# Expert weights split by ScalarE and VectorE alone

## Chip, core and metric

The kernel runs on one core of a Trainium2 chip. The metric is the device time of one execution in microseconds, the median of three runs. The engines are TensorE (PE; its weight loads are listed as PEld), VectorE (DVE), ScalarE (ACT), GpSimd (POOL) and SyncE (SP), which here issues most of the DMAs.

## What is computed

Three layers follow each other:

```python
# 1. attention of 2 batches, 8 heads, 768 tokens, 64 dims; a token sees those of its cluster
mask = q_assign[:, :, :, None] == k_assign[:, :, None, :]
scores = np.where(mask, scale * np.matmul(q, k.transpose(0, 1, 3, 2)), -1000000000.0)
attn_out = softmax(scores) @ v
# 2. dense layer, 1536 tokens, 512 -> 2048 -> 512
h = np.maximum(x @ w_in, 0.0)
x = h * h @ w_out
# 3. experts: N, D, E, F = (1536, 512, 8, 1024)
do_compute = x @ w_skip > 0
e_idx = np.argmax(xc @ w_gate, axis=1)          # xc: the selected tokens
h = np.maximum(xc[mask] @ w1[e], 0.0)           # mask: the tokens of expert e
y[mask] = gate_w[mask, None] * (h @ w2[e])
out[do_compute] = xc + y
```

The weights of layer 3, `w1` (8 x 512 x 1024) and `w2` (8 x 1024 x 512), are float32.

## The kernel before

Products are made in PE's float32r format from exact parts: an operand x is split into hi (x rounded to that format) and lo = x - hi, and a product is the sum of hi·hi, hi·lo and lo·hi. Every operand thus costs a cast and a subtract on some other engine. In the names, `wih` and `wil` are the two parts of a piece of w1, `woh` and `wol` those of w2; `xh`, `xl` belong to a tile's tokens and `hh`, `hl` to its hidden activations.

The attention and the dense layer come first. The last chunk of the dense layer's tokens is routed (top expert, gate, rank inside the expert; lines 828 to 900), which yields lists of token numbers per expert and the order of the experts. From there the experts' tiles run. There are nine tiles of 128 tokens, 0 to 8: tile 0 (called A) and tile 1 (B) belong to the fullest expert, and each of the others to one other expert. `place` (line 947) loads the number of each expert into a register of SP once it is known, and SP can then load that expert's weights.

A tile u goes through PE in this order (lines 1179 to 1195): `g1(u, 0)`, 12 matmuls of 512 columns for the first half of the hidden features; `g2(u-1, 1)`, the second half of the previous tile's output; four transposes of tile u's hidden activations; `g1(u, 1)`; four transposes of the next tile's tokens; `g2(u, 0)`; four transposes of the second half of the hidden activations. After each group of transposes `parts` (line 1021) splits the result: ACT casts it (line 1028), DVE subtracts (line 1029, one input in PSUM). PE needs the lo part with the third matmul of the next product but one. `finish` (line 1054) has DVE make the output rows (line 1056) and POOL scatter them (line 1058); `gather` (line 1013) has POOL clear a tile and fetch the next but one tile's tokens.

An expert's weights are prepared by `half_weights` (line 746), a generator, called two half-experts at a time (`econvert_to`, line 784) so that they are done about one tile ahead of their use: four tiles of parts of each kind take turns. An expert's weights come in eight loads of 512 KB (`fetch`, line 738), issued by SP into seven staging buffers (`st`, three of them, and `xc`, four pieces of the first two chunks and the later ones) as these come free, that is, when both subtracts of what lay there are done. For each load there is one cast of 128 x 1024 and two subtracts of 128 x 512:

```python
eng = ENGS[p][4 * kind + 2 * n + c // 2]
if eng[0] == "a":
    nc.scalar.copy(out=hi[:, c:c + 2], in_=st)
else:
    hi_pool(hi[:, c:c + 2], st)
for i in range(2):
    (nc.vector if eng[1] == "v" else nc.gpsimd).tensor_tensor(
        out=lo[:, c + i], in0=st[:, i], in1=hi.bitcast(F32)[:, c + i], op=ALU.subtract)
```

These are lines 759 to 766; `hi_pool` (line 137) is a multiplication by 1.0 on POOL. The table that `ENGS` holds (lines 41 to 43 and 728) has a pair of letters for each of an expert's eight loads: the engine of the cast (a for ACT, p for POOL) and that of the subtracts (v for DVE, p for POOL). `ENG0` is for the first expert, `ENG1` for the second, `ENG2` for the other six. PE's order is written out by hand in this part; those of ACT, DVE and POOL are set by the scheduler of the language, which takes the instructions as the program text yields them and moves them by its own estimate of when each can run. Every engine works through its own list strictly in order.

Of the kernel before, what the change touches and what calls it, by code (L numbers as in the profile page):

```python
# [16 lines left out]
BIG = float(2 ** 50)  # L17
# [23 lines left out]
ENG0 = ('av', 'pv', 'av', 'ap', 'av', 'ap', 'ap', 'ap')  # L41
ENG1 = ('av', 'ap', 'av', 'pv', 'av', 'ap', 'av', 'pv')
ENG2 = ('av', 'ap', 'av', 'pv', 'av', 'vv', 'av', 'pv')
# [9 lines left out]
def clustered_attention_moe(  # L53
# [14 lines left out]
    # Token s of a batch sits on partition s // TT of tile s % TT.  # L68
    # Every float32r product is made of exact parts, x = hi + lo.
# [10 lines left out]
    G = 384  # L80
# [26 lines left out]
    # tri[p, m] = 1 where p < m  # L107
    nc.gpsimd.affine_select(out=tri16, in_=ones16, pattern=[[1, 128]], compare_op=ALU.is_gt,
                            fill=0.0, base=0, channel_multiplier=-1)
    # first1[k, m] = 1 where k = m, -1 where k < m in the same group of C, times BIG for k's  # L110
# [17 lines left out]
    # a chunk of G tokens: the attention's output, transposed, then the moe's, by tokens  # L128
# [11 lines left out]
    # parts of the moe's weights, a quarter of the hidden features at a time  # L140
# [10 lines left out]
    def split64(hi, lo, srcs, shape):  # L151
        # float64 words (low, high) to float32, then to its two parts: the exponent is
        # clamped to float32's range and rebased (the shift drops its upper bits); 23 bits
        # of the mantissa stay
        st = stp.tile([128, 512, 2], I32, name="st")
        sv = st.rearrange("p (c f) w -> p c f w", c=shape[0])
        if pace:
            # the load waits for this step's hidden features
            nc.scalar.copy(out=st.bitcast(F32)[:, 0, 0:1], in_=pace[0][:, 0:1])
        for c, src in enumerate(srcs):  # L160
            nc.sync.dma_start(out=sv[:, c], in_=src)
        yield
        lw, hw = st[:, :, 0], st[:, :, 1]
        u = stg.tile([128, 512], I32, name="u")
        l3 = stg.tile([128, 512], I32, name="l3", bufs=1)
        uf = u.bitcast(F32)
        hf = st.bitcast(F32)[:, :, 1]
        nc.scalar.activation(out=uf, in_=hf, func=AF.Abs, scale=2.0 ** -48)
        yield
        nc.vector.tensor_scalar(out=uf, in0=uf, scalar1=2.0 ** -63, scalar2=122880.0 * 2.0 ** -48,  # L170
                                op0=ALU.max, op1=ALU.min)
        yield
        nc.vector.tensor_scalar(out=l3, in0=lw, scalar1=29, scalar2=None, op0=ALU.logical_shift_right)
        yield
        nc.vector.scalar_tensor_tensor(out=l3, in0=hw, scalar=-0x80000000, in1=l3,
                                       op0=ALU.bitwise_and, op1=ALU.bitwise_or)
        yield
        nc.vector.scalar_tensor_tensor(out=u, in0=u, scalar=3, in1=l3,
                                       op0=ALU.logical_shift_left, op1=ALU.bitwise_or)
        yield  # L180
        ufs = uf.rearrange("p (c f) -> p c f", c=shape[0])
        hi_pool(hi, ufs)
        yield
        nc.gpsimd.tensor_tensor(out=lo, in0=ufs, in1=hi.bitcast(F32), op=ALU.subtract)  # L184
        yield
# [28 lines left out]
    # ------------------------------------------------------------------ attention  # L214
    # the operands' tiles, which the moe's tokens take over
# [6 lines left out]
    def x_parts(ch):  # L222
        # of a chunk, in the place of operands
        t = [operand(nm) for nm in (("A", "B") if ch < 3 else ("vs", "vs"))]
        return [(i.rearrange("p t x d -> p (t x d)") if ch == 3 else i.rearrange("p a s -> p (a s)"))
                .rearrange("p (k c) -> p k c", k=KD) for i in t]
# [16 lines left out]
    # the first hidden features' products, which run in the attention's last waits  # L243
# [22 lines left out]
    with ExitStack() as actx:  # L266
# [32 lines left out]
        def centroid():  # L299
            # normalized rows, transposed to [(h % 2, d), (h, c)] with the other head  # L300
            # of a pair zero
# [3 lines left out]
            # rows of even heads go to columns 0-63, of odd heads to 64-127  # L305
# [41 lines left out]
        def split(nm, x, o, hi, lo, heads):  # L347
            # parts by the same partitions, to the operands' rows by DMAs
            rows = slice(64 * heads[0], 128)
            for c in (slice(0, 384), slice(384, 768)):  # L350
                hi_pool(hi[rows, c], x[rows, c])
                nc.gpsimd.tensor_tensor(out=lo[rows, c], in0=x[rows, c], in1=hi.bitcast(F32)[rows, c],
                                        op=ALU.subtract)
            hi, lo = hi.bitcast(F32), lo.bitcast(F32)
            for h in heads:
                r, t = slice(64 * h, 64 * h + 64), o[h].bitcast(F32)
                nc.sync.dma_start(out=t[0:64, 0], in_=hi[r])
                nc.sync.dma_start(out=t[64:128, 0], in_=(lo if nm == "q" else hi)[r])
                nc.sync.dma_start(out=t[0:64, 1], in_=(hi if nm == "q" else lo)[r])

        # Logits by [(q or k, half of the tokens, head, cluster), token], the four blocks of
        # 32 rows at once, then turned.
# [9 lines left out]
        # cluster of each token: one-hot of the first largest logit; the largest ones  # L372
        # are marked and turned, then a later one is taken out by an earlier one
# [25 lines left out]
        # operand rows: 0 or -1 for q, BIG or 0 for k  # L399
# [10 lines left out]
        def split_v(vs, vn):  # L410
            # blocks [hi, lo] of the even head, [lo, hi] of the odd
            for c in range(0, TT, 2):
                c = slice(c, c + 2)
                hi_pool(vs[:, c, 0::3, :], vn[:, c])
                nc.gpsimd.tensor_tensor(out=vs[:, c, 1:3, :], in0=vn[:, c], in1=vs.bitcast(F32)[:, c, 0::3, :],
                                        op=ALU.subtract)
# [3 lines left out]
        def prepare(n):  # L420
            # operands of a pair of heads, in steps of the tensor engine's part and the rest
# [30 lines left out]
        def prepare_first():  # L452
            # the first pair's: the first head's operands come from the engines, for no
            # wait for DMAs; some are in the weights' staging tiles, whose loads then follow
# [80 lines left out]
        def scales(n, c):  # L535
            # 1 / (sum + 1e-9) of the rows, each on the partitions of its head
# [75 lines left out]
        def warm(n):  # L612
            # keeps the tensor engine's clock up through the waits
            if n:
                wm = ps_v.tile([128, G], F32, name="av")
                for _ in range(4 * n):
                    nc.tensor.matmul(out=wm[:, 0:128], lhsT=ones16, rhs=ones16, start=True, stop=True)
# [83 lines left out]
    # ------------------------------------------------------------------ moe  # L701
# [18 lines left out]
    # The experts' tiles of 128 tokens: A and B are of the fullest expert by the tokens  # L720
    # of all chunks but the last, A with those tokens, B with more; then one of every
    # other expert, where expert 0 has the place of the fullest.
# [15 lines left out]
    def fetch():  # L738
        # loads ahead of the conversions, into the free staging tiles
# [6 lines left out]
    def half_weights(p, kind, n, src=None):  # L746
        # two parts of an expert's weights, a half of its hidden features
# [44 lines left out]
    # per token: its number - 4096 in two exact parts, and its gate in three  # L792
# [19 lines left out]
    def turn_x(T):  # L812
        # a tile of tokens goes out, and is turned for its logits
# [14 lines left out]
    def route(ch):  # L828
        # top expert, gate and rank in the expert of the selected tokens of a chunk
# [13 lines left out]
        else:  # L843
            # by [(tile, output), token], the tiles at once, then turned
# [57 lines left out]
    def ranks(ch, base=None):  # L902
        # one-hot of the ranks of a chunk's tokens
# [11 lines left out]
    def slots(ch, sum, so):  # L915
        # per expert and slot: the parts of the token of that rank, 0 if none
# [10 lines left out]
    def index(ix, g, sg):  # L927
        # tokens and gates from their parts
# [4 lines left out]
    def choose():  # L933
        # the fullest expert so far, and the order of the experts
# [19 lines left out]
    def pick(i, sum):  # L954
        # list of the chosen expert
# [5 lines left out]
    def early():  # L961
        # routing of all chunks but the last, where done tells which are finished
# [45 lines left out]
    # ------------------------------------------------------------------ tiles of an expert  # L1008
# [4 lines left out]
    def gather(u):  # L1013
        # A comes from the output's rows: the last chunk's have not gone to xd then
# [6 lines left out]
    def parts(src, name):  # L1021
        # transposed 128-column blocks of src, in two parts
# [39 lines left out]
    # ------------------------------------------------------------------ products of the moe  # L1062
# [66 lines left out]
    def base():  # L1129
        # the last chunk, its second products by tiles of tokens, then tile A  # L1130
# [45 lines left out]
    # ------------------------------------------------------------------ moe2  # L1176
# [20 lines left out]
    # further tiles of tokens, for as many as the experts have  # L1197
# [64 lines left out]
```

## Time and profile before

| what | before |
|---|---|
| median of 3 runs | 709.74 us (709.6 to 710.33) |
| profiled execution | span 706.3 us, 11310 instructions |
| PE, PEld busy | 658.8 us (93%), 569.4 us (81%) |
| DVE busy | 495.7 us (70%), 904 instructions |
| ACT busy | 395.7 us (56%), 825 instructions |
| POOL busy | 313.9 us (44%), 374 instructions |

The profiler's execution is one of its own; it is told by its span, from the first to the last instruction, and no other time is listed for it. It is 3.4 us below the median of the runs, which also holds what lies around the instructions. The page cuts the span in 40 slices of 17.7 us and gives each engine's busy share in tenths:

```profile
PE   7899999999999998999999999999998889869794
DVE  5688999999999997555347655322447789899960
POOL 4545453645635519344334344311002767665510
DMA  6678565565734101212221221012125969878700
```

The attention fills the first 16 or so slices, the dense layer those up to the 30th; the experts' tiles are in the last ten.

### The profile page before, as it was taken

How to read it: one execution, taken by the hardware profiler on the slowest of the kernel's cores; microseconds unless marked ns; L12 is line 12 of the kernel's file. 1: busy time of each engine (PE TensorE's matmuls, PEld its weight loads, DVE VectorE, ACT ScalarE, POOL GpSimd, SP SyncE). 2: the span in 40 equal slices, each digit the busy share in tenths (PEclk: the TensorE clock that was granted, in tenths of full speed). 3: DMA queues.
4: the chain of work that ended last, by engine and by line, in shares of the span. 5: the costliest groups of instructions: out<-in, count | busy, mean ns of one | idle time of the engine just before them, and what ended most of it. 6: DMA issues, size and time to landing. Idle time of an engine off the chain costs nothing. (4 is left out here: it accounts for less than half of the span.)

```text
span 706.3 us, 11310 instructions
## 1 busy us (share of the span) xinstructions
PE 658.8 (93%) x3769; PEld 569.4 (81%) x3769; DVE 495.7 (70%) x904; ACT 395.7 (56%) x825; POOL 313.9 (44%) x374
## 2 busy tenths in 40 slices
PE   7899999999999998999999999999998889869794
PEld 5688888889888887889998999899886768657583
DVE  5688999999999997555347655322447789899960
ACT  6688999989989884444433333223232736444420
POOL 4545453645635519344334344311002767665510
PEclk9999999999999999999999999999999989998998
DMA  6678565565734101212221221012125969878700
GB/s 140 149 167 199 140 148 147 123 148 141 168 95 113 31 0 47 67 60 75 87 75 64 75 82 61 1 45 90 60 85 180 343 217 360 291 242 279 249 26 23
DMA packets 72035, 89.91 MB, mean 127 GB/s; under 512 B 32384, under 2 KB 43584, under 8 KB 71968
## 3 DMA queue, kind: packets, MB, share of 16 engines
q1 hardware_dynamic: 69664, 84.52, 41.0%
q0 software_dynamic: 1440, 3.01, 1.3%
q10 hardware_dynamic: 864, 1.57, 0.6%
q8 instruction: 32, 0.52, 0.3%
q14 instruction: 35, 0.29, 0.1%
HBM read 62.18 MB, written 9.44 MB: 101 GB/s over the span
## 5 line engine op out<-in xcount | busy, mean ns | idle before, releaser
L580 DVE TENSOR_TENSOR pl<-pt,ph 128x384 fp32r<-128x384 f32 x192 | 103.7, 551 | 19.9 <-ACT ph L571 18.4
L557 PE MATMUL pt<-ident,p 128*128 128x128 f32 x576 | 96.6, 277 | 4.9 <-DVE pl L580 3.9
L259 ACT ACTIVATE r<-hps 128x384 f32<-128x384 f32 x62 | 30.4, 491 | 125.7 <-PE hps L252 125.5
L515 PE MATMUL sc<-B,A 80*128 80x384 f32 (+1 forms) x384 | 93.1, 363 | 4.7 <-ACT p L531 1.8
L138 POOL TENSOR_SCALAR hh<-r 128x384 fp32r<-128x384 f32 x62 | 35.0, 564 | 137.7 <-ACT r L260 118.6
L571 ACT CAST ph<-pt 128x384 fp32r<-128x384 f32 x192 | 89.7, 481 | 8.9 <-PE pt L557 8.5
L522 DVE TENSOR_REDUCE nm<-sc 128x1 f32<-128x768 f32 x96 | 91.0, 948 | 2.6 <-PE sc L515 2.6
L531 ACT ACTIVATE p<-sc,nm 128x768 f32<-128x768 f32 x96 | 87.3, 910 | 6.0 <-DVE nm L522 5.5
L262 DVE TENSOR_TENSOR hl<-r,hh 128x384 fp32r<-128x384 f32 x62 | 36.7, 591 | 76.9 <-POOL hh L138 76.9
L557 PEld LDWEIGHTS pt<-ident,p 128*128 128x128 f32 x576 | 70.3, 141 | 20.3 <-DVE pl L580 12.8
L1087 PE MATMUL acc<-woh,hh 128*128 128x512 f32 x186 | 74.2, 399 | 0.0
L1087 PE MATMUL acc<-woh,hl 128*128 128x512 f32 x186 | 73.3, 394 | 0.0
L1087 PE MATMUL acc<-wol,hh 128*128 128x512 f32 x186 | 73.3, 394 | 0.0
L590 PE MATMUL av<-ph,vs 128*128 128x384 f32 x192 | 73.1, 381 | 0.1
L515 PEld LDWEIGHTS sc<-B,A 80*128 80x128 f32 (+1 forms) x384 | 63.3, 191 | 9.9 <-ACT p L531 5.5
L590 PE MATMUL av<-pl,vs 128*128 128x384 f32 x192 | 65.4, 341 | 0.6 <-DVE pl L580 0.6
L252 PE MATMUL hps<-A,wil 128*128 128x384 f32 x184 | 62.0, 337 | 1.8 <-POOL wil L184 1.8
L252 PE MATMUL hps<-A,wih 128*128 128x384 f32 x184 | 62.4, 339 | 0.0
L252 PE MATMUL hps<-B,wih 128*128 128x384 f32 x184 | 62.0, 337 | 0.0
L1087 PEld LDWEIGHTS acc<-woh,hl 128*128 128x128 f32 x186 | 35.0, 188 | 8.0
L1087 PEld LDWEIGHTS acc<-woh,hh 128*128 128x128 f32 x186 | 35.0, 188 | 5.8 <-DVE xc L1095 0.2
L1095 DVE TENSOR_TENSOR xc<-acc,xc 128x512 f32<-128x512 f32 x36 | 24.4, 686 | 21.6 <-PE acc L1087 21.6
(268 smaller groups left out, 1549.4 us busy)
## 6 DMA issues: line engine op xcount, KB each, us to landing
xc<-in_moe_w_dram SPq DMA_DIRECT2D x34, 512.0 KB, 5.0
st<-in_moe_w_dram SPq DMA_DIRECT2D x30, 512.0 KB, 5.2
st<-in_moe_w_in_dram SPq DMA_DIRECT2D x64, 128.0 KB, 3.0
st<-in_moe_w_out_dram SPq DMA_DIRECT2D x16, 512.0 KB, 3.5
A<-hi SPq DMA_DIRECT2D x30, 192.0 KB, 3.1
B<-hi SPq DMA_DIRECT2D x30, 192.0 KB, 3.1
qn<-in_q_dram SPq DMA_DIRECT2D x16, 192.0 KB, 3.2
kn<-in_k_dram SPq DMA_DIRECT2D x16, 192.0 KB, 3.7
```

What stands on the lines that cost most here:

```text
L138: nc.gpsimd.tensor_scalar(out=o, in0=i, scalar1=1.0, scalar2=0.0, op0=ALU.mult, op1=ALU.add)
L252: nc.tensor.matmul(out=hps, lhsT=wi[w][:, c, f * 128:(f + 1) * 128], rhs=xhl[ch][a][:, c], start=(n == 0), stop=(n == 3 * KD - 1))
L259: nc.scalar.activation(out=r, in_=hps, func=AF.Relu)
L262: nc.vector.tensor_tensor(out=hl, in0=r, in1=hh.bitcast(F32), op=ALU.subtract)
L515: nc.tensor.matmul(out=sc[:, c, 0:384], lhsT=A[h][0:kk, a, t * 128:(t + 1) * 128], rhs=Bk[h][0:kk, a, c * 384:(c + 1) * 384], start=(a == ...
L522: nc.vector.tensor_reduce(out=nm_t[i], in_=sc_t[i][:, :, 0:384], op=ALU.max, axis=AX.XY, negate=True)
L531: nc.scalar.activation(out=p, in_=sc[:, :, 0:384], func=AF.Exp, bias=nm, scale=1.0, accum_out=su_t[n, c][:, t, h:h + 1])
L557: nc.tensor.transpose(out=pt[:, c], in_=p_t[i][:, n, c * 128:(c + 1) * 128], identity=ident)
L571: nc.scalar.copy(out=block(i, n)[by_pool].bitcast(F32) if by_pool else block(i, n)[0], in_=pt_t[i, n])
L580: nc.vector.tensor_tensor(out=pl, in0=pt_t.pop((i, n)), in1=ph.bitcast(F32), op=ALU.subtract)
L590: nc.tensor.matmul(out=av, lhsT=vs[:, c, 2 * h:2 * h + 2].rearrange("p x d -> p (x d)"), rhs=r[:, c], start=(c == 0 and i == 0), stop=(c = ...
L1087: nc.tensor.matmul(out=acc, lhsT=h2[a][:, i * 128:(i + 1) * 128], rhs=wo[w][:, f], start=(f == 0 and n == 0), stop=(f == NF - 1 and n == 2))
```

## The change

Every pair in the table becomes `'av'`: ACT makes all casts of the experts' weights and DVE all subtracts.

```diff
-ENG0 = ('av', 'pv', 'av', 'ap', 'av', 'ap', 'ap', 'ap')
-ENG1 = ('av', 'ap', 'av', 'pv', 'av', 'ap', 'av', 'pv')
-ENG2 = ('av', 'ap', 'av', 'pv', 'av', 'vv', 'av', 'pv')
+ENG0 = ('av',) * 8
+ENG1 = ('av',) * 8
+ENG2 = ('av',) * 8
```

(A pair `'vv'` in `ENG2` has its cast on POOL, since only `a` names another engine.) The rest of the diff takes comments out. In what is executed PE's list and SP's stay as they were; those of ACT, DVE and POOL change, and since the scheduler places the instructions anew, neighbours change places too.

On DVE, in the routing of the last chunk, between the largest logits and the ranks (`oh` is the one-hot of the expert, `gate` its probability, `cnt` the tokens per expert):

```order
 L865 TENSOR_REDUCE mr_6776<-oh_6773 128x3
+L765 TENSOR_TENSOR wol<-st,woh 128x512 x2
 L866 TENSOR_TENSOR oh_6773<-oh_6773,mr_6776 128x24
+L888 TENSOR_REDUCE gate<-ex 128x3
 L869 TENSOR_TENSOR oh_3989<-oh_6773,sel 128x24
-L888 TENSOR_REDUCE gate<-ex 128x3
 L889 TENSOR_SCALAR gate<-gate 128x3
-L890 RECIPROCAL gate<-gate 128x3
-L892 CAST vals<-gate 128x3
+L765 TENSOR_TENSOR wil<-xc_91,wih 128x512
+L1029 TENSOR_TENSOR hl<-xps,hh 128x512
 L883 COPY cnt<-rk 128x8
```

Weight subtracts now stand among the routing's small operations: from the first of them to `pay` on line 896 there are two in the list before and six in the new one, and one of line 1029 more ahead of `sgB` on line 925.

On ACT, in tile 1, whose hidden activations are `hs_6988` and, transposed and cast, `hh_7006`. Before:

```order
L1028 CAST xh_6971<-xps_6966 128x512
L1043 ACTIVATE hs_6988<-hps_6975 128x512
L761 CAST wih_7114<-xc1_92 128x1024
L1028 CAST hh_7006<-xps_7001 128x512
L761 CAST wih_7114<-st_5816 128x1024
L1043 ACTIVATE hs_7016<-hps_6994 128x512
```

And now:

```order
L1028 CAST xh_6971<-xps_6966 128x512
L1043 ACTIVATE hs_6988<-hps_6975 128x512
L761 CAST wih_7114<-xc1_92 128x1024
L761 CAST wih_7114<-st_5816 128x1024
L1028 CAST hh_7006<-xps_7001 128x512
L1043 ACTIVATE hs_7016<-hps_6994 128x512
```

The cast of the second load of the third expert (`wih_7114<-st_5816`) has moved ahead of `hh`.

On DVE, in one of the later tiles, from one row of output (`yo`) to the next; this is the new list:

```order
L1056 SCALAR_TENSOR_TENSOR yo_7227<-acc_7158,gp_4009,l3_5821 128x512
L765 TENSOR_TENSOR wol_7322<-xc1_92,woh_7321 128x512
L1029 TENSOR_TENSOR hl_7238<-xps_7232,hh_7237 128x512
L765 TENSOR_TENSOR wol_7322<-xc1_92,woh_7321 128x512
L765 TENSOR_TENSOR wol_7322<-st_5816,woh_7321 128x512 x2
L765 TENSOR_TENSOR wil_7377<-st_5817,wih_7376 128x512
L1029 TENSOR_TENSOR xl_7286<-xps_7280,xh_7285 128x512
L765 TENSOR_TENSOR wil_7377<-st_5817,wih_7376 128x512
L765 TENSOR_TENSOR wil_7377<-st_5818,wih_7376 128x512 x2
L765 TENSOR_TENSOR wil_7387<-xc2_93,wih_7386 128x512
L1029 TENSOR_TENSOR hl_7308<-xps_7302,hh_7307 128x512
```

Up to the next `yo` follow seven more weight subtracts, so that there are 16 in a tile; before there were 14, the other two being POOL's.

## Rows read from the trace of the kernel before

**Rows 1.** Windows, by stretch: busy us of PE, PEld, DVE, ACT and POOL, granted clock, DMA share, GB/s.

```profile
586.70:599.20 12.50, 12.50 (x64) 10.21 (x62) 11.92 (x19) 7.58 (x10) 8.20 (x7) 1.00 0.98 343
599.20:611.70 12.50, 10.05 (x41) 7.84 (x39) 9.96 (x13) 4.51 (x6) 6.92 (x6) 0.86 0.85 294
```

**Rows 2.** Timeline of PE: start us, busy us, what, [idle before and its releaser].

```profile
605.10 0.79 PE L1035 MATMUL acc<-woh,hl 128*128 128x512 f32 x1 [2.45 <-DVE hl L1029]
...
635.33 0.79 PE L1035 MATMUL hps<-wih,xl 128*128 128x512 f32 x1 [5.73 <-DVE xl L1029]
...
659.75 0.50 PE L1035 MATMUL acc<-woh,hl 128*128 128x512 f32 x1 [0.46 <-DVE hl L1029]
...
663.56 0.50 PE L1035 MATMUL hps<-wih,xl 128*128 128x512 f32 x1 [0.31 <-DVE xl L1029]
...
670.23 0.79 PE L1035 MATMUL acc<-woh,hl 128*128 128x512 f32 x1 [3.62 <-DVE hl L1029]
```

**Rows 3.** Timeline of ACT: first hidden activations of tiles 2, 3 and 8.

```profile
589.84 0.60 ACT L1043 ACTIVATE hs<-hps 128x512 f32<-128x512 f32 x1 [1.32 <-PE hps L1035]
...
602.30 0.60 ACT L1043 ACTIVATE hs<-hps 128x512 f32<-128x512 f32 x1 [1.31 <-PE hps L1035]
...
684.03 0.60 ACT L1043 ACTIVATE hs<-hps 128x512 f32<-128x512 f32 x1 [2.27 <-PE hps L1035]
```

**Rows 4.** Timeline of DVE: four subtracts in close order, and two long rows.

```profile
590.22 2.48 DVE L765 TENSOR_TENSOR wol<-xc,woh 128x512 fp32r<-128x512 f32 x4
592.63 0.74 DVE L1056 SCALAR_TENSOR_TENSOR yo<-acc,sB,u 128x512 f32<-128x512 f32 x1
...
629.16 5.52 DVE L765 TENSOR_TENSOR wil<-st,wih 128x512 fp32r<-128x512 f32 x1
...
663.42 6.15 DVE L765 TENSOR_TENSOR wil<-xc,wih 128x512 fp32r<-128x512 f32 x3
```

**Rows 5.** Timeline of POOL around the first of the long rows.

```profile
628.08 1.51 POOL L1017 DMA_INDIRECT u<-xd,ixp  x1 [0.17 <-POOL woh L138]
629.61 2.50 POOL L765 TENSOR_TENSOR wil<-xc,wih 128x512 fp32r<-128x512 f32 x2
...
633.09 1.04 POOL L138 TENSOR_SCALAR woh<-st 128x1024 fp32r<-128x1024 f32 x1
```

**Rows 6.** Windows of lines 765 (DVE, POOL), 761 (ACT), 138 (POOL), 1029 (DVE) alone.

```profile
541.00:698.00 157.00, 90.30 (x104) 34.97 (x24) 0.92 0.70 240
...
541.00:698.00 157.00, 44.44 (x43) 0.92 0.70 240
...
541.00:698.00 157.00, 24.29 (x21) 0.92 0.70 240
...
541.00:698.00 157.00, 18.47 (x27) 0.92 0.70 240
```

**Rows 7.** Timeline of DVE: routing of the last chunk.

```profile
558.17 0.95 DVE L862 SCALAR_TENSOR_TENSOR oh<-ex,rev 128x24 f32<-128x24 f32 x1
559.16 0.18 DVE L865 TENSOR_REDUCE mr<-oh 128x3 f32<-128x24 f32 x1
559.37 0.98 DVE L866 TENSOR_TENSOR oh<-oh,mr 128x24 f32<-128x24 f32 x1
560.38 1.19 DVE L869 TENSOR_TENSOR oh<-oh,sel 128x24 bf16<-128x24 f32 x1
...
564.79 1.23 DVE L894 TENSOR_TENSOR gate<-gate,vals 128x3 f32<-128x3 f32 x1
```

**Rows 8.** Timeline of PE: its wait for the routing.

```profile
567.88 0.28 PE L919 MATMUL sl<-pay,so 128*128 128x40 bf16 x3 [2.47 <-DVE pay L896]
```

**Rows 9.** Timelines of SP and DVE in tile 1; median us from a load to its landing.

```profile
575.67 2.87 SPq L743 DMA_DIRECT2D st<-in_moe_w_dram  x3
...
582.55 0.69 DVE L1029 TENSOR_TENSOR hl<-xps,hh 128x512 fp32r<-128x512 f32 x1
...
st<-in_moe_w_dram SPq DMA_DIRECT2D x30, 512.0 KB, 5.2
```

## Prediction

> **What bounds the kernel now.** I began with the page's 40 slices: the stage of the experts, from about 541 us on, is the one place where PE's digit falls while DVE's stays at its top, so the change (it touches nothing earlier) is judged there. The windows by stretch come next. In the stretch of tile 2 PE is busy for all of its 12.50 us at a granted clock of 1.00; in the next one it is busy for 10.05 of 12.50 at 0.86 [rows 1]. One tile of 128 tokens therefore costs PE about 12.5 us where nothing holds it up. The first hidden activations say the same more exactly: tile 2 has it at 589.84, tile 3 at 602.30, 12.46 us apart; tile 8 has it at 684.03 [rows 3]. Six tiles took 94.2 us where six times 12.46 is 74.8, so **19.4 us** are lost there.
>
> PE's timeline says to what. Three long waits, 2.45, 5.73 and 3.62 us, and smaller ones such as 0.46 and 0.31, all end with DVE's low parts of the activations, hl or xl on line 1029 [rows 2]. The three make 11.8 us. Most of the other 7.6 follows from them: 0.86 of full speed over 12.5 us means that 28% of it, 3.5 us, ran at 1.2 instead of 2.4 GHz, which costs 1.75 us behind the first wait alone [rows 1].
>
> Why was DVE late? Four weight subtracts in close order take 2.41 us to the start of the next instruction, 0.60 each; yet one of the same size took 5.52 us, and three took 6.15 [rows 4]. POOL's timeline answers for the first: from 628.08 to 634.13 (633.09 + 1.04) it ran four neighbours without a pause, the gather's issue, two subtracts and two casts of weights; the 5.52 us subtract ended at 634.68, one normal subtract after POOL stopped [rows 5]. Altogether DVE spent 90.30 us on 104 weight subtracts, 0.87 each [rows 6]. Routing shows the same stretch: three small operations that follow each other took 0.95, 0.98 and 1.19 us, with a like one of 0.18 among them, and a later one 1.23 [rows 7].
>
> **Which operations collide** can be read off too. The subtracts of line 1029, with one input in PSUM, took 18.47 us for 27, 0.68 each: unstretched, though POOL was at work throughout [rows 6]. The Trainium skill, page "SBUF — State Buffer", section "Who interferes with whom", says that a DVE instruction with two SBUF inputs contends with a GpSimd instruction that reads SBUF, one with at most one such input does not, and that the loser waits until the other instruction finishes. By that rule the trace agrees about the operations, not about the length: DVE stayed out through a whole run of POOL's instructions, not one. The sum below goes by the rows; what the shorter contention would leave is a rival.
>
> **The change, part by part.** POOL loses 24 subtracts (34.97 us) and 21 casts (24.29 us) [rows 6]; it keeps gathers, scatters and memsets. ScalarE gets the 21 casts at 44.44/43 = 1.03 us, 21.7 us in all; DVE gets the 24 subtracts at 0.60, 14.4 us [rows 4, 6]. DVE's own 104 fall from 90.3 to about 104 x 0.60 = 62.4, so its subtract time goes to 128 x 0.60 = 76.8: shorter by 13.5 us although there are more of them. PE's order in what is executed, and SP's, do not change.
>
> *Tiles 2 to 8: -19.4.* Whether all of the loss comes back depends on what each engine needs per tile beside PE's 12.46. DVE: 16 weight subtracts x 0.60, three of line 1029 x 0.68, one output row of 0.74, 12.4 us [rows 4, 6]. ScalarE: 8 x 1.03 plus five passes over 512 columns at 0.60, 11.2 [rows 3, 6]. DMA: eight loads of 512 KB, 4.19 MB, at the 343 GB/s of the undisturbed tile, whose DMA share was 0.98, 12.2 [rows 1, 9]. All fit, none with much to spare. The cover is that the weights are prepared a whole tile ahead; the new order on DVE puts four weight subtracts between hl and xl, four between xl and the next hl, seven ahead of the output row, which is about how PE's own work falls between those points.
>
> *New small waits: +1.5.* With DVE at 12.4 of 12.46 some hl will come late. Nothing in the trace prices that: below, 0; above, each subtract costs its 0.68 alone instead of 0.60 in close order, 16 x 0.68 + 2.04 + 0.74 = 13.7, which is 1.24 us a tile and 7.4 in six. I take 1.5, twice the 0.46 + 0.31 of the small waits of now [rows 2], since the order leaves room.
>
> *Routing and tile 1: -1.0.* The stretch on the way to pay goes: 0.95 + 0.98 + 1.19 + 1.23 less four times 0.18 is 3.6 us [rows 7]. But four more weight subtracts now stand ahead of pay, 2.4 us. That leaves about 1 us, for PE's wait for pay (2.47) and for the expert numbers that SP needs for its next loads [rows 8]. More is not kept: ScalarE's cast of the second load of expert 2 now stands ahead of hh of tile 1. That load is issued at 575.67 and lands by the median 5.2 us later, at 580.9; then cast 1.03, hh 0.60 and hl 0.69 end at 583.2, as hl does today (582.55 + 0.69) [rows 3, 6, 9]. So tile 1 moves only as far as the loads do, 1 us. Bounds: the wait of 2.47 vanishes with as much clock as behind the first long wait, -4.2; or the new wait in tile 1 costs as much as the shortest long one, 2.45 + 1.75 = +4.2 [rows 1, 2].
>
> Sum: -19.4 + 1.5 - 1.0 = -18.9. The profiled span of 706.3 us becomes 687.4. The median of the three runs is 709.74; the 3.4 us between span and median stay, and the forecast is **690.8 us**.
>
> **Rivals.** *DVE becomes the bound* (0.15): it is 11.92 us busy of 12.50 even in the undisturbed tile [rows 1], partly stretched. With each subtract at 0.68 the +1.5 becomes +7.4: 696.7 us. For it: the 12.4 of 12.46. Against it: subtracts in close order are what rows 4 show when casts are ready. [...]
>
> *Late loads hold up ScalarE's queue* (0.07, slower). hh and xh, which PE needs soon, now stand behind two or three casts, each waiting for its load; with DMA at 0.98 [rows 1] a load can land after its cast's turn, and hh, hl and PE wait for it. It decides once a tile loses more than 20.4/6 = 3.4 us. At the shortest long wait with its clock, 4.2 us, six tiles lose 25.2: 709.74 - 20.4 + 25.2 = 714.5 us. Against it: seven staging buffers keep loads about a tile ahead.
>
> *Only part of the stretch is POOL's* (0.03, faster by little). If each of the three long waits owes POOL one instruction, at most a subtract of 1.25 us (half of 2.50) [rows 5], and the rest a cause that stays, 3.8 us come back: 709.74 - 3.8 = 705.9 us. The end of the 5.52 us row, just behind POOL's last instruction and not its first, speaks against it. By the Trainium skill's rule above, where the loser waits for one instruction, this is the case.
>
> *The stretch is not POOL's at all* (0.02, slower): then DVE's 24 new subtracts cost 0.87 too, 20.9 us, on an engine without slack: about 730. Rows 4 and 5, with ends that coincide, speak against it. Part gains and losses that cancel (0.03) would leave the time where it is.
>
> **How the numbers follow.** The forecast has 0.70, the rivals 0.15, 0.07, 0.03 and 0.02, and 0.03 is left for no change, by which I mean within 0.2% (1.4 us), about what a measurement can tell. Faster is 0.70 + 0.15 + 0.03 = 0.88, slower 0.07 + 0.02 = 0.09. The range goes from all lower bounds, 709.74 - 19.4 - 4.2 = 686, to all upper ones, 709.74 - 19.4 + 4.2 + 7.4 = 702; it holds the forecast and the DVE rival and leaves out 0.15.
>
> **What would show it.** Right: DVE's weight subtracts 128 at about 0.68 each in the trace with none over 1 us; the routing's small operations at 0.18; first hidden activations of tiles 2 to 8 about 12.5 us apart and PE's clock at 1.00 there; pay no more than 2 us earlier. DVE as the bound: even tile distances near 13.7, with PE waiting for hl or xl behind weight subtracts of normal length. Loads as the bound: ScalarE's casts ended by DMA, with PE's waits behind hh. Wrong altogether: long subtracts with POOL idle.

## The result and the profile after

| | before | after |
|---|---|---|
| median | 709.67 us of 4 runs (708.45 to 710.33) | 688.4 us of 4 runs (686.96 to 690.47) |
| profiled span | 706.3 us | 686.5 us |

The ratio is 0.9715, its 95% interval 0.9684 to 0.9746: 2.9% faster. The forecast was 690.8 us, with a range of 686 to 702.

The page after, parts 1 and 2 (busy us with their share of the span; busy tenths in 40 slices):

```profile
span 686.5 us, 11273 instructions
...
PE 655.3 (95%) x3769; PEld 569.2 (83%) x3769; DVE 481.0 (70%) x928; ACT 415.1 (60%) x846; POOL 253.0 (37%) x329
...
PE   7889999999999999899999999999999898999994
...
POOL 4534555536365445644344453421110203113110
...
DMA  6567565655655200213212222101222596999900
```

DVE made 24 instructions more in 14.7 us less (481.0 against 495.7). PE's digits of the last ten slices, once 8889869794, are now 9898999994: from tile 2 on, 9 up to the last slice.

The six tiles from tile 2's first hidden activations to tile 8's, timeline of ACT, as in [rows 3]:

```profile
589.87 0.60 ACT L1043 ACTIVATE hs<-hps 128x512 f32<-128x512 f32 x1 [0.48 <-PE hps L1035]
...
602.31 0.60 ACT L1043 ACTIVATE hs<-hps 128x512 f32<-128x512 f32 x1
...
664.75 0.60 ACT L1043 ACTIVATE hs<-hps 128x512 f32<-128x512 f32 x1 [2.28 <-PE hps L1035]
```

74.88 us instead of 94.19, so 19.31 us came back here. Tile 2 itself starts at the same time as before (589.87 against 589.84); everything is decided behind it.

The same stretch as a window, of the kernel before and then of the one after (length; busy us of PE, PEld, DVE, ACT and POOL; granted clock; DMA share; GB/s). Before:

```profile
589.84:684.03 94.19, 81.63 (x362) 64.11 (x361) 82.97 (x103) 41.77 (x56) 52.08 (x42) 0.93 0.71 241
```

After:

```profile
589.87:664.75 74.88, 74.88 (x362) 61.36 (x361) 67.69 (x111) 55.82 (x73) 14.95 (x16) 1.00 0.85 303
```

PE's 362 matmuls are the same. Before, it was idle for 94.19 - 81.63 = 12.56 us; now it is busy for the whole of the stretch, at a clock of 1.00. What the clock took before stands in the windows of the kernel before that follow the three long waits of [rows 2]:

```profile
605.10:608.00 2.90, 2.90 (x7) 2.32 (x8) 2.90 (x5) 0.00 (x0) 0.00 (x0) 0.50 0.66 216
635.40:640.00 4.60, 4.60 (x12) 3.63 (x13) 4.60 (x8) 0.20 (x1) 0.00 (x0) 0.58 0.65 213
670.30:675.00 4.70, 4.70 (x17) 3.76 (x18) 3.59 (x7) 0.28 (x1) 0.00 (x0) 0.67 0.30 109
```

In them PE is busy all the time, the first at the lower of its two levels (1.2 of 2.4 GHz), the others partly so. At full clock their work would have taken 2.90 x 0.50 + 4.60 x 0.42 + 4.70 x 0.33 = 4.9 us less. So of the 19.31 us, 12.56 were PE's idle time and about a quarter, 4.9, the low clock behind the three long waits. The other 1.8 us are busy time of PE as well; these windows do not show where they come from.

What PE still waits for among the experts' tiles, table of waits from 541 us on (us in all, times, longest):

```profile
PE xps L1025 <- DMA u<-out_dram,ixA: 2.6, 1, 2.6
PE sl L919 <- DVE pay L896: 1.1, 1, 1.1
...
PE rk L873 <- DVE oh L869: 0.5, 1, 0.5
...
PE hps L1035 <- DVE xl L1029: 0.2, 1, 0.2
```

The waits of [rows 2] for hl and xl are gone but for 0.2 us, which lie ahead of tile 2; pay's has shrunk from 2.47 [rows 8] to 1.1.

Line 765 on DVE, line 761 on ACT and line 1029 on DVE alone, windows as in [rows 6]:

```profile
541.00:698.00 157.00, 80.95 (x128) 0.95 0.69 244
...
541.00:698.00 157.00, 65.40 (x64) 0.95 0.69 244
...
541.00:698.00 157.00, 18.45 (x27) 0.95 0.69 244
```

A weight subtract now costs 80.95/128 = 0.63 us of DVE where it cost 90.30/104 = 0.87. As single rows the 128 lie between 0.665 and 0.732 us; of the 104 before, 18 were over 1 us. Line 1029's 27, with one input in PSUM, have not changed (18.47 before).

### The profile page after: what moved, and what is told of

Its sections match the earlier page's. It is cut to its first block, busy times and chain, and to the rows that moved or that the text cites. A ratio compares the mean times of both kernels' runs of the same rounds, so it can differ in the third digit from the quotient of the medians.

```text
span 686.5 us, 11273 instructions
## 1 busy us (share of the span) xinstructions
PE 655.3 (95%) x3769; PEld 569.2 (83%) x3769; DVE 481.0 (70%) x928; ACT 415.1 (60%) x846; POOL 253.0 (37%) x329
## 5 line engine op out<-in xcount | busy, mean ns | idle before, releaser
L580 DVE TENSOR_TENSOR pl<-pt,ph 128x384 fp32r<-128x384 f32 x192 | 103.5, 550 | 19.8 <-ACT ph L571 18.3
L138 POOL TENSOR_SCALAR hh<-r 128x384 fp32r<-128x384 f32 x62 | 36.5, 589 | 137.9 <-ACT r L260 118.8
L1087 PEld LDWEIGHTS acc<-wol,hh 128*128 128x128 f32 x186 | 35.3, 190 | 5.3
```

Source lines behind the costliest of these rows:

```text
L138: nc.gpsimd.tensor_scalar(out=o, in0=i, scalar1=1.0, scalar2=0.0, op0=ALU.mult, op1=ALU.add)
L580: nc.vector.tensor_tensor(out=pl, in0=pt_t.pop((i, n)), in1=ph.bitcast(F32), op=ALU.subtract)
L1087: nc.tensor.matmul(out=acc, lhsT=h2[a][:, i * 128:(i + 1) * 128], rhs=wo[w][:, f], start=(f == 0 and n == 0), stop=(f == NF - 1 and n == 2))
```

## The experiments

Three theories were set against each other. **T1:** GpSimd instructions that read SBUF stretch VectorE's subtracts of two SBUF inputs. **T2:** GpSimd is a slow stage in the chain from load to product, and others wait for what it hands on. **T3:** the scheduler's new order of the lists does it, whatever GpSimd does.

Ten kernels ran, each timed beside runs of the kernel before, to which the ratios refer. The main ones in one table: the median, and of each profile the length of the six tiles and DVE's weight subtracts (busy us from 541 to 698, number, single ones over 1 us, the longest):

| kernel | median us | ratio to before | six tiles us | subtracts on DVE |
|---|---|---|---|---|
| before | 709.67 | | 94.19 | 90.30, 104, 18, 5.52 |
| after | 688.4 | 0.9715 (0.9684 to 0.9746) | 74.88 | 80.95, 128, 0, 0.73 |
| only the casts on GpSimd | 701.1 | 0.9903 (0.9884 to 0.9922) | 83.56 | 93.86, 128, 15, 2.04 |
| only the subtracts on GpSimd | 699.52 | 0.988 (0.9861 to 0.9899) | 78.99 | 76.88, 104, 12, 1.80 |
| after + reading work on GpSimd | 696.28 | 0.9821 (0.98 to 0.9842) | 81.26 | 91.80, 128, 11, 1.23 |
| after + memsets on GpSimd | 690.95 | 0.9736 (0.9707 to 0.9765) | 74.76 | 81.03, 128, 0, 0.77 |

**One part undone at a time.** First only GpSimd's casts come back:

```diff
-ENG1 = ('av',) * 8
-ENG2 = ('av',) * 8
+ENG1 = ('av', 'av', 'av', 'pv', 'av', 'av', 'av', 'pv')
+ENG2 = ('av', 'av', 'av', 'pv', 'av', 'pv', 'av', 'pv')
```

(and in `ENG0` the second pair becomes `'pv'`).

> GpSimd makes the 21 casts again that it made before (24.3 us of its time), and none of the subtracts; TensorE's and SyncE's lists stay. If GpSimd's reading of SBUF holds up VectorE's subtracts (T1), long subtracts come back on VectorE, each beside a GpSimd cast, and the loss is about the casts' part of GpSimd's weight work, 24.3 of 59.3 us, so 8 of the 20 us: about 696 us. If what cost time was GpSimd as one more stage that hands weights on late (T2), the subtracts after its casts start late but stay near 0.68 us each, and TensorE waits for the weights' parts (wil, wol), not for the activations' lo parts: 692 to 700 us. If the gain came from the scheduler's new order of the lists alone (T3): about 688 us, as this order is mostly the new one.

701.1 us, 12.7 more than the changed kernel, where 8 were guessed. Its six tiles as a window, around 619 us the rows of DVE and of POOL (start, us), and PE's waits in the six tiles:

```profile
589.28:672.84 83.56, 77.73 (x362) 60.42 (x361) 79.16 (x114) 41.71 (x56) 39.39 (x32) 1.00 0.81 272
...
618.38 3.33 DVE L765 TENSOR_TENSOR wol<-xc,woh 128x512 fp32r<-128x512 f32 x4
...
619.04 1.53 POOL L138 TENSOR_SCALAR woh<-st 128x1024 fp32r<-128x1024 f32 x1 [2.33 <-PE xps L1025]
...
PE acc L1035 <- DVE hl L1029: 4.2, 7, 1.0
PE hps L1035 <- DVE xl L1029: 1.5, 1, 1.5
```

Four subtracts took 3.33 us where they take 2.48 undisturbed [rows 4]; one of them ran from 619.58 to 621.11, until 0.54 us after POOL's cast of another load ended. In the six tiles PE waits for hl (4.2 us in seven waits, the longest 1.0) and xl (1.5 in one), and for no weights: T1's signs, not T2's. Of the loss, 8.7 us lie in the six tiles, about as guessed. The profile has 2.7 more behind tile 8: there GpSimd stands still for 3.0 us after its last scatter has landed, and no row gives a reason.

Then only the subtracts:

```diff
-ENG0 = ('av',) * 8
-ENG1 = ('av',) * 8
-ENG2 = ('av',) * 8
+ENG0 = ('av', 'av', 'av', 'ap', 'av', 'ap', 'ap', 'ap')
+ENG1 = ('av', 'ap', 'av', 'av', 'av', 'ap', 'av', 'av')
+ENG2 = ('av', 'ap', 'av', 'av', 'av', 'av', 'av', 'av')
```

> GpSimd makes the 24 subtracts again that it made before (35.0 us of its time), and none of the casts. T1: 35.0 of 59.3 us, so 12 of the 20 us come back: about 700 us, with subtracts of VectorE of over 1 us and the activations' lo parts late at TensorE. VectorE has 24 subtracts fewer to do, which would gain nothing as its time in a tile is already below TensorE's. T2: TensorE waits for lo parts of the weights that GpSimd made, and VectorE's own subtracts stay at 0.68 us. T3: about 688 us.

699.52 us, as expected, though only 4.1 us of it lie in the six tiles. Tile 2 also starts 3 us later (592.84): half of the 24 subtracts belong to the first two experts, and PE waits 2.4 us for tile 1's xl. Another 2.4 us lie behind tile 8, as in the run before. The window, and DVE's and POOL's rows around 602 us:

```profile
592.84:671.83 78.99, 76.17 (x362) 60.82 (x361) 71.28 (x101) 55.82 (x73) 33.13 (x26) 1.00 0.82 286
...
601.90 3.08 DVE L765 TENSOR_TENSOR wil<-st,wih 128x512 fp32r<-128x512 f32 x2 [0.35 <-ACT wih L761]
...
601.00 3.44 POOL L765 TENSOR_TENSOR wil<-st,wih 128x512 fp32r<-128x512 f32 x2 [1.54 <-ACT wih L761]
```

Both engines are stretched: DVE's two take 1.54 each on average, POOL's two 1.72, where POOL's ran at 1.25 in [rows 5] while DVE was held out. They take turns. The two parts lose 8.7 + 4.1 = 12.8 us in the six tiles, the kernel before lost 19.31. Of the 6.5 us between them, 4.9 are the clock shown above: with half of the work PE's longest wait in these tiles is 1.5 us and the granted clock stays at 1.00 in both windows.

**Work on GpSimd that nobody waits for.** This tells T1 from T2 and T3 at once: no data and no order changes, only GpSimd is busy. In the first form the work depended on nothing:

```diff
+was = WAS[p][4 * kind + 2 * n + c // 2]
+for i in range(4 * (was[0] != 'a')):
+    hi_pool(scr, scr)
+for i in range(4 * (was[1] == 'p')):
+    nc.gpsimd.tensor_tensor(out=scr3, in0=scr3, in1=slot2, op=ALU.subtract)
```

`WAS` is the table of before, `scr` a scratch tile of 128 x 256, `scr3` a view of it, `slot2` a constant.

> The changed kernel, and beside it GpSimd does work that nobody needs or waits for, at the places where it used to make weights: on a scratch tile, four multiplications of 128 x 256 for each former cast and four subtracts of 128 x 256 for each former pair of subtracts. No instruction of another engine is moved or made to wait. T1: VectorE's weight subtracts stretch again although nothing depends on GpSimd (mean well above 0.68 us, single ones of 2 to 6 us), tiles stand more than 12.5 us apart, and most of the loss is back: 698 to 710 us. T2 and T3: about 688 us, VectorE's subtracts at 0.68 us.

> The same as the run before it, but what GpSimd does beside is only clearing of the scratch tile (four memsets of 128 x 256 for a former cast, nine for a former pair of subtracts), which writes SBUF and reads nothing. T1 in its form that reading is what interferes: about 688 us, VectorE's subtracts at 0.68 us. If any work of GpSimd interferes, written bytes too: as long as the run with reads, 698 to 710 us. T2 and T3: about 688 us.

736.23 and 713.19 us, both slower than before, and neither says anything on the question: the scheduler, which saw no input to wait for, put the work some 300 us earlier, into the attention and the dense layer (all memsets stand between 226 and 341 us). There GpSimd makes parts that others need at once. The waits of the first of the two between 200 and 360 us (us, times, longest):

```profile
DVE hl L263 <- POOL hh L139: 22.0, 6, 7.0
...
PE pt L558 <- DVE pl L581: 15.3, 7, 5.9
```

So the work was tied to its place, with one column of the freshly cast weights read at the head of each group:

```diff
+if was[0] != 'a' or was[1] == 'p':
+    nc.gpsimd.tensor_copy(out=scr[:, 0:1], in_=hi.bitcast(F32)[:, c, 0:1])
```

> The work on GpSimd that nobody waits for, now tied to the place of the weights it once made: each group begins with a copy of one column of the cast weights (wih or woh) into the scratch tile, so that the scheduler can't move it ahead of the load. The lists of TensorE, ScalarE, VectorE and SyncE are those of the changed kernel, instruction for instruction. T1 (GpSimd's reading of SBUF holds up VectorE): subtracts of VectorE of 2 us and more come back among the experts' tiles, tiles stand more than 12.5 us apart, 698 to 712 us. T2 (GpSimd as a slow stage that others wait for) and T3 (order of the lists): 688 us, VectorE's subtracts at 0.68 us. The attention stays as in the changed kernel in all cases.

> As the run before it, with the same copy of one column at the head of each group, but then only memsets of the scratch tile, which read nothing. T1 as stated (it is the reading): 688 to 690 us, VectorE's subtracts at 0.68 us. If any use of SBUF by GpSimd does it, as slow as the run with reads. T2 and T3: 688 us.

722.63 and 693.49 us. Long subtracts are back in the first, but it overdid it: GpSimd's two kinds of work took 49.0 and 47.3 us where the casts and subtracts had taken 24.3 and 35.0, so its gathers were late as well. PE's waits in it:

```profile
PE xps L1037 <- DMA u<-xd,ixB: 7.4, 1, 7.4
PE xps L1037 <- DMA u<-xd,ixp: 6.4, 2, 4.0
```

The run with memsets had such a wait too, 5.7 us for tile B's tokens, ahead of tile 2. So a third pair left the first two experts alone (`WAS` has `'av'` there), and in the run with reads GpSimd had less to do, two multiplications or three subtracts a group (the memsets stayed at four and nine):

> As e3b_pool_reads_tied, but only for the experts from the third on (tiles 2 to 8), and with about the time that GpSimd spent there before: two multiplications of 128 x 256 (0.58 us each in the last run) for a former cast, three subtracts (0.99 us each) for a former pair. This leaves GpSimd free to fetch the tokens of tiles A and B in time, which the last run's 7.4 us wait of TensorE for B's tokens says it was not. The lists of the other engines are again the changed kernel's. T1: tile 2's hs at 590 us as in the changed kernel; long subtracts come back; the loss is below that of the two runs with weights back on GpSimd (12.7 and 11.1 us) together, as its instructions are short and VectorE gets in between them: 692 to 702 us. T2 and T3: 688 us.

> As e4b_pool_memsets_tied, only for the experts from the third on: four memsets (0.31 us each) for a former cast, nine for a former pair of subtracts, so about the same time of GpSimd as in the run beside it. The last such run had tiles 2 to 8 at 12.46 us each and lost its time ahead of them, to the late tokens of tile B. T1: now nothing is left of that, 688 to 689 us. If writing interferes too: tiles over 12.5 us apart. T2 and T3: 688 us.

696.28 and 690.95 us. With reads, the window of the six tiles, the rows of DVE and POOL around 601 us, and DVE's weight subtracts alone:

```profile
591.96:673.22 81.26, 77.04 (x362) 60.54 (x361) 77.55 (x112) 56.76 (x73) 65.08 (x85) 1.00 0.79 274
...
600.03 3.67 DVE L766 TENSOR_TENSOR wil<-st,wih 128x512 fp32r<-128x512 f32 x4
...
600.92 3.37 POOL L776 TENSOR_TENSOR scr<-scr,slot 128x256 f32<-128x256 f32 x3
...
541.00:698.00 157.00, 91.80 (x128) 0.95 0.69 244
```

With memsets, the same (line 766 is the weight subtract here, too):

```profile
594.42:669.18 74.76, 74.76 (x362) 61.12 (x361) 67.43 (x111) 55.86 (x72) 57.71 (x150) 1.00 0.82 298
...
607.28 1.89 DVE L766 TENSOR_TENSOR wol<-xc,woh 128x512 fp32r<-128x512 f32 x3
...
606.87 1.42 POOL L774 MEMSET scr<- 128x256 f32 x4
...
541.00:698.00 157.00, 81.03 (x128) 0.94 0.68 244
```

The lists of PE, ACT, DVE and SP are those of the changed kernel in both, and GpSimd is busy for 65 or 58 us of the stretch; the work put in is 39 us of that with reads and 35 us with memsets, about what the weights took there before (52.08 - 14.95 = 37 us). Reading stretches DVE's subtracts (91.80 us for 128) and lengthens the six tiles by 6.4 us; writing alone does neither (81.03 us; 0.63 each, beside POOL's memsets). Every subtract of over 1 us, the 18 of before and the 15, 12 and 11 of the runs with casts, subtracts and reading work, overlaps an instruction of GpSimd that reads SBUF. This **shows T1**, and it rules T3 out as the whole: with the changed kernel's order and GpSimd reading, a third of the 19.31 us is lost again. The run with memsets has its median 2.5 us above the changed kernel's, but the two overlap (687.98 to 694.11 and 686.96 to 690.47); its profile, of the slowest execution, is longer by 4.6 us ahead of tile 2 and 1.4 behind tile 8, and not in the tiles.

One part of T1 rests on rows alone. No run brought back a subtract of about 5 us: the longest in any of them is 2.04. Before, there were two, of 5.52 and 4.95 us, and behind them lie PE's two longest waits, 5.73 and 3.62 of the 12.56 us. The first is in [rows 4, 5]; the second ran from 663.42 to 668.37, beside these two instructions of POOL and two casts directly behind them, which ended at 667.82:

```profile
663.27 2.53 POOL L765 TENSOR_TENSOR wil<-xc,wih 128x512 fp32r<-128x512 f32 x2
```

T2 has a small part that was not separated. In the six tiles of before DVE waited 4.2 us in all for casts by GpSimd (2.9 for woh, 1.3 for wih), in the run with only casts 0.7; PE never waited for a weight's part in the tiles.

**How near DVE is to being the bound.** One subtract in four is made twice (for every second load, the first of its two):

```diff
+if c:
+    nc.vector.tensor_tensor(out=lo[:, c], in0=st[:, 0], in1=hi.bitcast(F32)[:, c], op=ALU.subtract)
```

> The changed kernel with every second pair of subtracts made into three (the last is made once more, the result is the same): 32 subtracts more on VectorE, four in a tile. VectorE's need in a tile becomes about 11.8 + 4 x 0.68 = 14.5 us, over TensorE's 12.5 us. If VectorE is near to being the bound in the changed kernel (the rival at 696.7 us had this as its point): tiles 2 to 8 stand 14.5 us apart, about 12 us more, 700 us. If VectorE has more room than its sum of busy times tells (its waits are only for others' results): less than that, 690 us or so, and the first sign is the waits of TensorE for hl and xl.

699.3 us, ratio 0.9862 (0.9834 to 0.9891): 10.9 us more than the changed kernel, about as expected of a bound. Window of the six tiles:

```profile
594.26:675.97 81.71, 77.05 (x362) 60.54 (x361) 77.75 (x130) 57.48 (x72) 20.91 (x16) 1.00 0.82 276
```

A tile takes 13.6 us, not 14.5. DVE's work grew by 77.75 - 67.69 = 10.1 us and the stretch by 6.8; PE's waits there are almost all for xl (3.8 us in three). Tile 2 also starts 4.4 us later, with PE's wait for oh up from 0.5 to 3.5 us. In the changed kernel DVE is busy for 67.69 of 74.88 us of this stretch, but not evenly. Windows of it from one tile's first hidden activations to the next one's, of tiles 3, 5 and 7:

```profile
602.31:614.82 12.51, 12.51 (x62) 10.22 (x61) 12.24 (x21) 10.21 (x13) 2.59 (x3) 1.00 1.01 363
...
627.27:640.18 12.91, 12.91 (x63) 10.58 (x62) 12.64 (x21) 10.22 (x13) 2.58 (x3) 1.00 1.01 358
...
652.23:664.75 12.52, 12.52 (x62) 10.24 (x61) 8.02 (x13) 5.68 (x9) 1.02 (x1) 1.00 0.05 17
```

From tile 3 to tile 6 DVE is busy for 98% of the time and the DMA engines for all of it (shares of 1.01 and 1.02); in the last window there are few weights left to prepare. So DVE is all but the bound in the changed kernel, although PE waits for nothing there, and 10 us more make PE wait.

**Fewer loads in flight.** With `HOLD = 1` instead of 2, part of the staging room is handed to the loads only after the routing:

> The changed kernel with HOLD = 1: one piece of the staging room, of two 512 KB loads, is handed to the experts' loads only after the last chunk's routing, so that fewer loads are in flight when GpSimd fetches the tokens of tile A, for which TensorE waits 2.61 us at the stage's start. If those loads are what delays the fetch: that wait shrinks, and up to 2.6 us are gained, 686 us. If the loads are needed early: ScalarE and VectorE get the second expert's weights later and TensorE waits for wil or wol in tile 2, 690 to 695 us. If neither: 688 us.

689.54 us, ratio 0.974 (0.9703 to 0.9778), which can't be told from the changed kernel. The wait for A's tokens stayed, here in PE's timeline:

```profile
546.83 0.78 PE L1025 MATMUL xps<-ident,u 128*128 128x128 f32 x4 [2.51 <-DMA u<-out_dram,ixA]
```

The loads held back are not needed so early, then. Whether loads are what makes that gather late stays open: in the 7 us before its tokens came, the DMA share was 0.93 in this run and 0.92 in the changed kernel, so DMA had no less to do. No run here pointed to a version that beats the changed kernel, and with PE, DVE and DMA all but full from tile 3 to tile 6 there is little room for one there.

## Why the prediction was right

The main step held, down to its size: *tiles 2 to 8, -19.4*, measured -19.31. The reading behind it was that GpSimd is what makes DVE late. The two runs that give half of its work back and the run with reading work show it for the subtracts of up to 2.04 us, and the one with memsets shows that reading is what matters; for the two subtracts of about 5 us it stays a reading of rows. The prediction miscounts these rows: its *four neighbours* without a pause are five instructions, a gather's issue, two subtracts and two casts, and DVE's subtract began during the first, 0.45 us ahead of the other four. The choice of operations that collide was right as well: line 1029 stayed at 0.68 us in every kernel.

*New small waits, +1.5*: measured +0.1 (74.88 less six times 12.46). DVE's need was sized rightly, 12.4 us against 11.8 to 12.6 in tiles 3 to 6. What did not follow is that so full a DVE makes PE wait: the new order has each low part made in time. ScalarE needed 10.2 us a tile, not 11.2, and DMA, worked out as 12.2 us at 343 GB/s, was busy all the time at 358 to 372.

*Routing and tile 1, -1.0*: about -1.2, hidden by something else. The routing's small operations fell to 0.18 and 0.15 us from the 0.95 to 1.23 of [rows 7]:

```profile
561.06 0.18 DVE L862 SCALAR_TENSOR_TENSOR oh<-ex,rev 128x24 f32<-128x24 f32 x1
...
562.57 0.18 DVE L866 TENSOR_TENSOR oh<-oh,mr 128x24 f32<-128x24 f32 x1
...
566.62 0.15 DVE L894 TENSOR_TENSOR gate<-gate,vals 128x3 f32<-128x3 f32 x1
```

But this profiled execution came some 1.2 us later to the experts' stage, which the change doesn't touch (a pair of loads is issued at 541.41, before at 540.17), and so tile 2 starts as before. In tile 1 it went as worked out, with ACT's hh behind the cast of a load of expert 2. ACT in tile 1 before, then SP, ACT and DVE after:

```profile
580.15 0.60 ACT L1043 ACTIVATE hs<-hps 128x512 f32<-128x512 f32 x1 [3.46 <-PE hps L1035]
...
575.94 1.65 SPq L743 DMA_DIRECT2D st<-in_moe_w_dram  x3
...
579.51 0.60 ACT L1043 ACTIVATE hs<-hps 128x512 f32<-128x512 f32 x1 [3.67 <-PE hps L1035]
...
581.51 1.05 ACT L761 CAST wih<-st 128x1024 fp32r<-128x1024 f32 x1 [0.47 <-DMA st<-in_moe_w_dram]
582.47 0.58 ACT L1028 CAST hh<-xps 128x512 fp32r<-128x512 f32 x1
...
583.20 0.68 DVE L1029 TENSOR_TENSOR hl<-xps,hh 128x512 fp32r<-128x512 f32 x1
```

The load landed at 581.49 and the cast waited for it; hl started at 583.20 where it was 582.55 [rows 9]. So tile 1's first hidden activations came 0.64 us earlier than before, its hl 0.65 later, and tile 2 at the same time. Tile 0's had come 2.7 us later than before (559.84 against 557.16), so the term is made of larger parts that cancel, and that it came so near is in part luck. The rest of the span, behind tile 8, was 0.5 us shorter (21.75 against 22.27). Together: -19.31 - 1.2 + 1.2 - 0.5 = -19.8 us of span, where -18.9 was forecast.

The median fell by 21.3 us. Of the 3.4 us between span and median that the forecast kept, only about 1.7 are fixed: so much lies the time above the span in every run here. The execution profiled before was thus itself some 1.7 us faster than the median. That, and not the terms, is most of the 2.4 us between 690.8 and 688.4.

**The rivals.** *DVE becomes the bound*: PE did not wait for it in the changed kernel, though it is at 98% from tile 3 to tile 6; with 10.1 us more of DVE work in the six tiles PE did. *Late loads hold up ScalarE's queue*: ACT did wait for loads, 1.4 us in three waits in tile 1 and 0.5 us in one in the six tiles, and PE for none of it; DMA moved 303 GB/s in the six tiles where it had moved 241. *Only part of the stretch is POOL's* was mispriced, though it did not occur. It took what one held-up instruction costs from the three long waits alone, 3.8 us. In the runs with half of GpSimd's work nearly every held subtract lost its place to one instruction of POOL, not a run of them, and that costs 12.8 us in the six tiles. Beside these, the whole runs of POOL [rows 4, 5] were two cases of the 18 in before; they lie ahead of its two longest waits, 5.73 and 3.62 us [rows 2]. The rule of the Trainium skill, "SBUF — State Buffer", section "Who interferes with whom", that the loser waits for one instruction, fits most rows, then, and the prediction spoke too strongly against it. The same section says that a GpSimd instruction which only writes SBUF does not contend; the run with memsets agrees (0.63 us a subtract).

## What to carry to other kernels

Before work is handed to GpSimd to relieve VectorE, look at the inputs of what VectorE runs meanwhile: here 24 subtracts and 21 casts taken off it and ScalarE cost more than they gave, since VectorE's subtracts with both inputs in SBUF went from 0.63 to 0.87 us on average beside them. What counts is the late low part at TensorE, and the clock that is low behind its long waits, not the sum of busy time: the run with only the casts on GpSimd had more VectorE time in its subtracts than before (93.86 us for 128 against 90.30 for 104) and still lost less. And an instruction that depends on nothing recent has no place of its own: a scheduler may move it to where it hurts.

## What was not expected of the hardware

- The two engines can take turns, and then both pay: VectorE's subtract took 1.54 us on average instead of 0.68, GpSimd's 1.72 instead of 1.25. In two cases of the kernel before, VectorE's subtract got no turn and was held for 5.52 and 4.95 us, through four instructions of GpSimd, which ran at full speed. VectorE's two began within half a microsecond of the first of the four, and each time these came directly behind the issue of a gather; why VectorE got no turn stays open, as no run tried it.
- Memsets on GpSimd, 35 us of them in 75, cost VectorE's subtracts nothing (0.63 us each).
- Losses do not add up: either half of GpSimd's work left the granted clock of the six tiles at 1.00, both halves together went with 0.93, and behind three waits that cost 4.9 us more.
